# Two layers twice on one core: two tiles of the first layer norm transposed by DMA, halved weight loads, and a newly searched order

## The chip, the core and the metric

The kernel runs on one core of one Trainium2 chip. A core has a matrix engine (TensorE, PE in the profile), a vector engine (VectorE, DVE), a scalar engine (ScalarE, ACT), GpSimd (POOL) and SyncE (SP), which here issues every DMA. The engines run side by side, each through its own list of instructions in order, and wait for each other by semaphores. The metric is the device time of one execution in microseconds (us). Three runs of the kernel before gave 267.95, 268.95 and 270.68 us, a median of 268.95.

## The reference

`x` is 2048 rows of 512 bf16 values. The same two residual layers run twice over:

```python
x = x + _A_ref(_layernorm(x), A_wqkv, A_wo)   # linear attention, 32 heads of 16
x = x + _B_ref(_layernorm(x), B_w1, B_w2)     # relu(x @ w1) @ w2, inner size 1376
x = x + _A_ref(_layernorm(x), A_wqkv, A_wo)
x = x + _B_ref(_layernorm(x), B_w1, B_w2)
```

In `_A_ref`, q, k and v come from one product with `wqkv`. With `phi(t) = where(t > 0, t + 1, exp(t)) + 1e-6`, each head forms `kv = phi(k)^T v` and the sum `z` of `phi(k)` over all rows; the output is `phi(q) kv / (phi(q) z)`, times `wo`. As `kv` and `z` sum over all rows, the second half of a layer A can begin only when the first half has seen every row.

## The kernel before, in words

The 2048 rows are 16 tiles of 128 rows, four tiles to a chunk (`t` = 0 to 3). Layers are numbered 0 to 3 (A, B, A, B), and each layer is a list of steps by chunk; steps of the next layer are woven in when the rows that they need are there. Activations stay in SBUF from the first load to the last store, and so do all weights.

Before a projection a tile is normalised into `xn` (row by row) and then transposed into `Tb`, which has the 512 values of a row along the partitions, in four blocks `c` of 128. There are two ways to transpose. `transpose_pe` has PE multiply four 128x128 blocks by the identity into PSUM (line 600 in the profile), and ACT (line 606) or DVE (line 607) copies the result to `Tb`. `transpose_half` issues one DMA transpose for a pair of tiles on SP's queue (line 586). In layer 0, tiles 0 to 7 go the first way and tiles 8 to 15 the second; in all other layers all tiles go by DMA. In layer B the last 96 columns of the inner activations, `hr`, are also turned by a DMA transpose (`trh`, line 826).

At the start of layer 0, `ln_stats_first` forms mean and variance of a tile on DVE (`bn_stats`, line 534, and `bn_aggr`, line 535); `ln_part_first` makes 1/sqrt(variance), on ACT (lines 540 and 542, Ln and Exp) for tiles 0 to 3 and for the groups of four tiles, on DVE and POOL (lines 545 and 547) for tiles 4 to 7; `ln_norm` writes `xn` on DVE (line 572). `ones_col` then sets the last column of `xn` to 1 on POOL (line 665), since products with `xn` also yield the sums over rows. `warm` issues eight matmuls on zeros before any data is there (line 503), and `warm_fill` four small ones behind the PE transposes of tiles 0 and 1 (line 529). All products of real data stand under line 635, where one helper issues matmul groups.

`a_k(i)` is the K projection of tile i: four matmuls of 512 columns, one for each block `c` of the contraction. `a_q` projects a chunk for q; for chunk 0 `a_q_half` does this in two halves of two tiles each, in 256 columns. `phi` of a projection takes two passes of ACT over PSUM (line 618 linear, line 620 exponential) and two of DVE (lines 622 and 628). `g_r` and `g_a` are products of `phi(k)` with `xn`. `wv_less_last` takes the last row of wv from the rest (DVE, line 661).

Loads are issued by SP in the order of its list: x tiles 0, 1, 2 to 3, then wk (the columns of `wqkv` for k, 512 KB), x 4 to 7, wq, x 12 to 15, x 8 to 11, wv and its last row `wvl`, `wo`, `w1`, and after the first two DMA transposes `w2`. One semaphore belongs to each DMA, so that a user of wk waits for the whole of it.

The order of every engine's list is made by a planner when the kernel is built. `_list_schedule` walks through time with a fixed duration for each operation and picks, within a window of each engine's list, the operation that can start first; ties go by `prio`, the place in the program plus an entry of the table `HINTS`. An entry whose key ends in `!` fixes the engine of an operation that could run on several (`add_flex`). For a DMA the planner takes an issue time on SP's queue (`C_SP_ISSUE`, `C_LOAD_ISSUE`, 1350 ns for `transpose_half`), then 1400 ns, a transfer on one shared channel, 600 ns and an extra `late`. The planner's times decide the order alone; on the chip each instruction waits for its semaphores.

Of the kernel before, what the change touches and what calls it, by code (L numbers as in the profile page):

```python
# [16 lines left out]
C_MM512 = 216.0  # L17
# [26 lines left out]
C_SP_ISSUE = 60.0  # L44
# [10 lines left out]
HINTS = {"0.bnag8": 129, "0.bnst11": -246, "0.bnst12": 104, "0.bnst13": 129, "0.bnst14": 143, "0.bnst15": 144, "0.bnst6": -4,  # L55
# [56 lines left out]

# [1273 lines left out]
```

## Time and profile before

| what | value |
|---|---|
| median of three runs | 268.95 us |
| profiled execution | 268.93 us |
| its span, first to last instruction | 267.2 us |
| around the span | 1.73 us |
| granted TensorE clock | 1.00 |
| PE busy | 262.0 us (98%) |
| DVE busy | 226.2 us (85%) |
| ACT busy | 187.0 us (70%) |
| POOL busy | 58.5 us (22%) |
| first matmul on data (a transpose), first projection | 4.96 us, 6.73 us |
| last matmul starts, last instruction | 263.90 us, 267.2 us |

Busy is the time in which an engine has at least one instruction running. The profile models the end of a matmul, so two matmuls in a row overlap in it; the distance from start to start is what a matmul costs. In a row of a timeline stand the start, the time that the group covers, the engine, the line of the kernel, the operation, the tile written and the tiles read, and how many instructions the row joins; in brackets comes idle time before it and what ended it. In rows of line 635 the first of the tiles read is the one streamed through the array: `ps<-wqkv,Tb` with 512 columns is a K projection, `ps<-Tb,wqkv` a q projection, `ps<-big,xn` belongs to the g products, `ps<-Tb,w` and `ps<-w,Tb` are the first products of layer B. SPq is SP's queue, where a DMA's row is the time that it takes to issue, not to land.

### The profile page before, as it was taken

What the parts mean: (1) busy time and instruction counts of PE and PEld (TensorE: products, weight loads), DVE (VectorE), ACT (ScalarE), POOL (GpSimd) and SP (SyncE); (2) the same over time, 40 slices, a digit from 0 to 9 for tenths busy, and PEclk for the clock granted to TensorE, in tenths of its full rate; (3) what the DMA queues carried; (4) which work ended last, traced back from release to release, by engine and by line L of the source; (5) the groups of instructions that cost most, each with busy time, mean ns of one, the idle gap of its engine ahead of it and who ended that gap; (6) DMA issues with size and microseconds to landing.
All of it is one profiled execution on the core that took longest, in us unless ns stands there. A gap on an engine that the chain in (4) does not pass through costs nothing.

```text
span 267.2 us, 5481 instructions
## 1 busy us (share of the span) xinstructions
PE 262.0 (98%) x2020; PEld 183.1 (69%) x2020; DVE 226.2 (85%) x636; ACT 187.0 (70%) x408; POOL 58.5 (22%) x146
## 2 busy tenths in 40 slices
PE   7999999999989999999999999999999999999995
PEld 3664547644745798857768755674488789888884
DVE  5799974789888999997998675459999999899994
ACT  4998896766975237999667797787899936057400
POOL 3210000026682001403103430000744434000000
PEclk9999999999999999999999999999999999999999
DMA  7986620763765000400400421054373223402003
GB/s 205 368 285 137 197 42 3 157 146 65 86 120 98 2 20 2 89 11 2 79 2 0 79 54 28 2 129 108 62 153 68 39 39 101 81 0 72 28 34 126
DMA packets 44890, 22.18 MB, mean 83 GB/s; under 512 B 34784, under 2 KB 43328, under 8 KB 44864
## 3 DMA queue, kind: packets, MB, share of 16 engines
q1 hardware_dynamic: 44864, 21.83, 34.3%
q8 instruction: 16, 0.26, 0.4%
q14 instruction: 10, 0.08, 0.1%
HBM read 7.14 MB, written 2.10 MB: 35 GB/s over the span
## 4 chain that ended last, share of the span: by engine, by line
PE 92%; ACT 3%; DMA 3%; DVE 1%; SPq 0%; issue 0%; DVEq 0%
PE ps L635 91%; ACT sqscr L650 2%; DMA Tb<-xn 2%; DMA xin<-in_A_x_dram 1%; PE ps L600 1%; ACT xn L581 1%; DVE xres L642 0%; DVE bst L534 0%; PE ps L529 0%; DVE rdc L1064 0%; SPq L471 0%; DVEq L1324 0%; DVE xn L572 0%; ACT big L946 0%
## 5 line engine op out<-in xcount | busy, mean ns | idle before, releaser
L618 ACT ACTIVATE big<-ps 128x512 bf16<-128x512 f32 x64 | 40.7, 644 | 9.5 <-PE ps L635 9.4
L650 ACT ACTIVATE sqscr<-xres 128x512 bf16<-128x512 f32 x48 | 30.0, 625 | 9.1 <-DVE xres L642 5.1
L635 PE MATMUL ps<-Tb,w 128*128 128x256 f16 (+1 forms) x216 | 35.3, 304 | 0.0
L635 PE MATMUL ps<-w,big 128*128 128x256 bf16 (+1 forms) x256 | 32.4, 272 | 0.0
L635 PE MATMUL ps<-wqkv,Tb 128*128 128x512 bf16 x128 | 31.2, 379 | 0.0
L635 PE MATMUL ps<-big,xn 128*128 128x256 bf16 (+1 forms) x224 | 31.1, 288 | 0.0
L635 PE MATMUL ps<-Tb,wqkv 128*128 128x512 f16 (+1 forms) x144 | 30.8, 355 | 0.0
L620 ACT ACTIVATE escr<-ps 128x512 bf16<-128x512 f32 x48 | 29.6, 634 | 1.1 <-PE ps L635 1.1
L635 PE MATMUL ps<-Mf,big 128*128 128x512 bf16 x128 | 29.6, 379 | 0.0
L635 PEld LDWEIGHTS ps<-w,big 128*128 128x128 bf16 (+1 forms) x256 | 24.9, 98 | 3.6 <-ACT big L946 0.3
L635 PEld LDWEIGHTS ps<-big,xn 128*128 128x128 f16 x224 | 21.3, 98 | 8.5 <-issue 0.8
L635 PEld LDWEIGHTS ps<-Tb,w 128*128 128x128 bf16 x216 | 20.6, 98 | 8.8 <-DMA Tb<-xn 0.4
L908 ACT ACTIVATE escr<-ps 128x512 f32<-128x512 f32 (+1 forms) x40 | 20.3, 544 | 8.1 <-PE ps L635 7.4
L895 DVE TENSOR_TENSOR big<-ps,escr 128x512 bf16<-128x512 f32 (+1 forms) x40 | 23.6, 603 | 1.7 <-ACT escr L908 1.1
L564 POOL TENSOR_TENSOR rstd<-veps,nhalf 128x2 f32<-128x2 f32 x24 | 20.4, 853 | 7.9 <-DVE veps L562 6.8
L635 PEld LDWEIGHTS ps<-Tb,wqkv 128*128 128x128 bf16 x144 | 13.7, 98 | 11.7 <-ACT escr L620 0.3
L635 PEld LDWEIGHTS ps<-Mf,big 128*128 128x128 bf16 x128 | 12.3, 98 | 13.8 <-ACT Mf L717 0.2
L622 DVE TENSOR_SCALAR escr<-escr 128x512 bf16<-128x512 bf16 x48 | 13.7, 289 | 8.6 <-ACT escr L620 8.4
L635 PEld LDWEIGHTS ps<-wqkv,Tb 128*128 128x128 f16 x128 | 12.2, 98 | 12.4 <-ACT Tb L606 0.4
L628 DVE TENSOR_TENSOR big<-big,escr 128x512 bf16<-128x512 bf16 x48 | 19.8, 419 | 0.8 <-ACT big L618 0.2
L581 ACT ACTIVATE xn<-xres,nbias,rstd 128x512 f16<-128x512 f32 x21 | 16.8, 815 | 5.1 <-DVE nbias L566 3.9
L898 ACT ACTIVATE big<-big 128x512 bf16<-128x512 bf16 (+1 forms) x31 | 16.2, 542 | 4.8 <-DVE big L895 4.7
(116 smaller groups left out, 515.9 us busy)
## 6 DMA issues: line engine op xcount, KB each, us to landing
big<-rdc SPq DMA_DIRECT2D x32, 128.0 KB, 2.7
wqkv<-in_A_wqkv_dram SPq DMA_DIRECT2D x3, 512.0 KB, 7.0
xin<-in_A_x_dram SPq DMA_DIRECT2D x3, 512.0 KB, 7.8
w<-in_B_w_dram SPq DMA_DIRECT2D x1, 1376.0 KB, 14.5
w<-in_B_w_dram SPq DMA_DIRECT2D x1, 1280.0 KB, 7.0
wo<-in_A_wo_dram SPq DMA_DIRECT2D x1, 512.0 KB, 10.3
out_dram<-GT SPq DMA_DIRECT2D x1, 512.0 KB, 4.1
out_dram<-Mf SPq DMA_DIRECT2D x1, 512.0 KB, 2.6
```

Of the source, the lines that this page charges most:

```text
L564: g.add(POOL, lambda e: e.tensor_tensor(rstd[:, sl], veps[:, sl], nhalf[:, 0:n], ALU.pow), [("veps", lo), ("nhalf",)], [("rstd", i) for i ...
L581: (ACT, lambda e: e.activation(xn[:, i, :], src, ACTF.Identity, scale=rstd[:, i:i + 1], bias=nbias[:, i:i + 1]), C_ACT_SB_AP)],
L600: last = e.transpose(psb()[:, 128 * c:128 * c + 128], xn[:, i, 128 * c:128 * c + 128], ident[:])
L618: g.add(ACT, lambda e: e.activation(dst_ap, psv[:, b, :], ACTF.Identity, bias=1.0 + 1e-6, scale=1.0), [("ps", b)], [dst_key], C_ACT_PSUM, ...
L620: g.add(ACT, lambda e: e.activation(sap, psv[:, b, :], ACTF.Exp), [("ps", b)], skeys, C_ACT_EXP, name=name + "_exp")
L622: g.add(DVE, lambda e: e.tensor_scalar(sap, sap, 1.0, 1e-6, ALU.min, ALU.add), skeys, skeys, C_DVE_BF4X, name=name + "_em")
L628: g.add(DVE, lambda e: e.tensor_tensor(dst_ap, dst_ap, sap, ALU.max), [dst_key] + skeys, [dst_key], 340.0, name=name + "_phi")
L635: last = e.matmul(o, l, r, start=st, stop=sp, skip_group_check=skip)
L650: g.add(ACT, lambda e: e.activation(sqscr[:, q, :], xres[:, i, :], ACTF.Square, scale=math.sqrt(INV_D), accum_out=s2[:, i:i + 1]), xr(i), ...
L895: g.add(DVE, lambda e: e.tensor_tensor(ap, sh(psv[:, bank, 0:w]), sh(other()), ALU.add), [("ps", bank)] + okeys + ([] if first else bk), q ...
L898: g.add_flex([(ACT, lambda e: e.activation(ap, ap, ACTF.Relu), C_ACT_PSUM if len(cs) == 2 else 270.0), (DVE, lambda e: e.tensor_scalar(ap, ...
L908: g.add(ACT, lambda e, w=w: e.activation(q[:, 0:w], psv[:, bank, 0:w], ACTF.Identity), [("ps", bank)], key, C_ACT_PSUM if len(cs) == 2 els ...
```

## The change

- In layer 0, tiles 6 and 7 are no longer transposed by PE. They are normalised as a pair, 1/sqrt(variance) by Ln and Exp on ACT, and one DMA transpose turns both. It is the first transpose and so the one that waits for the loads in `ALL_LOADS` too.
- The second `warm_fill` is left out.
- wk and wq are loaded in two halves of the contraction each (blocks 0 and 1, blocks 2 and 3). The K projections of tiles 0 and 1 and all parts of `a_q_half` become two matmul groups, each waiting for its own half.
- The loads of wv and `wvl` wait for `xn` of tiles 6 and 7, and those of `wo`, `w1` and `w2` for `xn` of tiles 12 to 15.
- The first normalisation of tiles 1 to 7 may be planned on POOL.
- In the planner, the default issue time on SP's queue is 450 ns instead of 60, and that of the transposes of `hr` is 1250 ns; two `late` values differ, and the load times of the halves are half of the whole.
- `HINTS` is another table (474 entries instead of 368), so that the lists of all engines in all four layers are in a new order.

```diff
-C_SP_ISSUE = 60.0
+C_SP_ISSUE = 450.0
+C_TR_ISSUE = 1250.0
...
-         "0.den1": 279, "0.fin12_0": -290, "0.fin13_0": -222, "0.fin6_0": -340, "0.g0_0_3": 73, "0.g0_2_3": 126, "0.g0_3_3":
+         "0.k6_em": -3, "0.k8_phi": -93, "0.k9_phi": 209, "0.kproj9": -485, "0.ld_wka": -100, "0.ld_wkb": -100, "0.ld_wqa":
+         -100, "0.ld_wqb": -99, "0.ld_wvl": 86, "0.ld_x0": -100, "0.ld_x1": -100, "0.ld_x12": -101, "0.ld_x2": -100, "0.ld_x4":
...
-        def ld_w(sl, key):
+        def ld_w(sl, key, cs=slice(0, 4)):
+            dma(lambda e: e.dma_start(wqkv[:, cs, sl], wq_v[:, cs, sl]), [], [(key,)], 370.0 * (cs.stop - cs.start), "ld_" + key,
+                issue=C_LOAD_ISSUE, late=700.0 if key[:2] == "wk" else C_LATE)
...
-        ld_w(slice(D, 2 * D), "wk")
+        ld_w(slice(D, 2 * D), "wka", slice(0, 2))
         ld_x(2, 4)
-        ld_w(slice(0, D), "wq")
+        ld_w(slice(D, 2 * D), "wkb", slice(2, 4))
+        ld_w(slice(0, D), "wqa", slice(0, 2))
+        ld_w(slice(0, D), "wqb", slice(2, 4))
...
+        def tied(load, names):
+            n = len(g.ops)
+            load()
+            for o in g.ops[n:]:
+                o.sdeps += [p for p in g.ops[:n] if p.name in names and p not in o.sdeps]
+
+        def loads_a():
...
+        def loads_b():
...
-            if hi <= FIRST_ACT_TILES or hi - lo == 4:
+            if hi <= FIRST_ACT_TILES or hi - lo >= 2:
...
-                g.add(DVE, lambda e: e.tensor_scalar(xn[:, i, :], xin[:, i, :], mv[:, i, 0:1], rstd[:, i:i + 1], ALU.subtract, ALU.mult),
-                      [("xin", i), ("mean", i), ("rstd", i)], [("xn", i)], C_DVE_NORM_BF, name="norm%d" % i)
+                f = (lambda e: e.tensor_scalar(xn[:, i, :], xin[:, i, :], mv[:, i, 0:1], rstd[:, i:i + 1], ALU.subtract, ALU.mult))
+                g.add_flex([(DVE, f, C_DVE_NORM_BF)] + ([(POOL, f, C_POOL_NORM)] if 0 < i < 8 else []),
+                           [("xin", i), ("mean", i), ("rstd", i)], [("xn", i)], name="fnorm%d" % i)
...
-            if i < 2:
+            if i < 1:
                 warm_fill(i)
...
+            parts = ((0, 1, "wka"), (2, 3, "wkb")) if first_k and i < 2 else ((0, 1, 2, 3, "wka", "wkb"),)
...
+                for k, key in enumerate(("wqa", "wqb")):
...
-                [("hr", s)], [("big", u)], 450.0, "trh%d" % t)
+                [("hr", s)], [("big", u)], 450.0, "trh%d" % t, issue=C_TR_ISSUE)
...
-                if t < FIRST_PE_CHUNKS:
+                if t < FIRST_PE_CHUNKS and i < 6:
...
+            if t == 1:
+                ln_part_first(6, 8)
+                ln_norm(6, True)
+                ln_norm(7, True)
+                tr_dma(1, 1)
...
+            if t == 1:
+                tied(loads_a, ["fnorm6", "fnorm7"])
...
+                        if t + 3 == NCH - 1:
+                            tied(loads_b, ["fnorm%d" % i for i in range(NT - 4, NT)])
```

More of the change, by code (lines that the diff above doesn't have):

```diff
@@ L52 @@
 WINDOW = {PE: 64, ACT: 80, DVE: 80, POOL: 12, SP: 6}
-HINTS = {"0.bnag8": 129, "0.bnst11": -246, "0.bnst12": 104, "0.bnst13": 129, "0.bnst14": 143, "0.bnst15": 144, "0.bnst6": -4,
[56 rows of a table removed]
+HINTS = {"0.bnag15": 26, "0.bnag3": 137, "0.bnag9": 130, "0.bnst12": 51, "0.bnst13": 223, "0.bnst15": 189, "0.bnst3": -18,
[80 rows of a table added]
 class _Op:
@@ L465, in ld_x @@
             dma(lambda e: e.dma_start(xin[:, lo:hi, :], x_v[:, lo - 1:hi - 1, :]), [], [("xin", i) for i in range(lo, hi)],
-                350.0 * (hi - lo), "ld_x%d" % lo, issue=C_LOAD_ISSUE, late={1: 100.0, 2: 200.0}.get(lo, C_LATE))
+                350.0 * (hi - lo), "ld_x%d" % lo, issue=C_LOAD_ISSUE, late={1: 100.0, 2: 650.0}.get(lo, C_LATE))
         wq_v = A_wqkv.rearrange("(c p) n -> p c n", p=128)
-        def ld_w(sl, key):
-            dma(lambda e: e.dma_start(wqkv[:, :, sl], wq_v[:, :, sl]), [], [(key,)], 1480.0, "ld_" + key, issue=C_LOAD_ISSUE, late=500.0 if key == "wk" else C_LATE)
+        def ld_w(sl, key, cs=slice(0, 4)):
+            dma(lambda e: e.dma_start(wqkv[:, cs, sl], wq_v[:, cs, sl]), [], [(key,)], 370.0 * (cs.stop - cs.start), "ld_" + key,
+                issue=C_LOAD_ISSUE, late=700.0 if key[:2] == "wk" else C_LATE)
@@ L471, in build_kernel @@
         dma(lambda e: e.dma_start(xin[:, 0, :], x_h), [], [("xin", 0)], 370.0, "ld_x0", issue=C_LOAD_ISSUE, late=-350.0)
         ld_x(1, 2)
-        ld_w(slice(D, 2 * D), "wk")
+        ld_w(slice(D, 2 * D), "wka", slice(0, 2))
         ld_x(2, 4)
-        ld_w(slice(0, D), "wq")
+        ld_w(slice(D, 2 * D), "wkb", slice(2, 4))
+        ld_w(slice(0, D), "wqa", slice(0, 2))
+        ld_w(slice(0, D), "wqb", slice(2, 4))
         for t in range(1, NCH):
             ld_x(4 * t, 4 * t + 4)
-        ld_w(slice(2 * D, 3 * D), "wv0")
@@ L479, in build_kernel @@
-        dma(lambda e: e.dma_start(wvl[:], A_wqkv[D - 1:D, 2 * D:3 * D].broadcast_to([128, D])), [], [("wvl",)], 2000.0, "ld_wvl",
-            issue=C_LOAD_ISSUE)
-        dma(lambda e: e.dma_start(wo[:], A_wo.rearrange("(c p) n -> p c n", p=128)), [], [("wo",)], 1500.0, "ld_wo", issue=C_LOAD_ISSUE)
         nfull = NFC - 1 if FLAST < 128 else NFC
-        dma(lambda e: e.dma_start(w1[:], B_w1.rearrange("(c p) n -> p c n", p=128)), [], [("w1",)], 4500.0, "ld_w1", issue=C_LOAD_ISSUE)
-        dma(lambda e: e.dma_start(w2[:, 0:nfull, :], B_w2[0:nfull * 128, :].rearrange("(c p) n -> p c n", p=128)),
-            [], [("w2a",)], 5500.0, "ld_w2a", issue=C_LOAD_ISSUE)
@@ L487, in build_kernel @@
-        if FLAST < 128:
-            dma(lambda e: e.dma_start(w2[0:FLAST, NFC - 1, :], B_w2[nfull * 128:DFF, :]), [], [("w2b",)], 600.0, "ld_w2b", issue=C_LOAD_ISSUE)
+        def tied(load, names):
[4 more added lines that the diff above has]
+        def loads_a():
+            ld_w(slice(2 * D, 3 * D), "wv0")
+            dma(lambda e: e.dma_start(wvl[:], A_wqkv[D - 1:D, 2 * D:3 * D].broadcast_to([128, D])), [], [("wvl",)], 2000.0, "ld_wvl",
+                issue=C_LOAD_ISSUE)
@@ new lines, in loads_b @@
+        def loads_b():
+            dma(lambda e: e.dma_start(wo[:], A_wo.rearrange("(c p) n -> p c n", p=128)), [], [("wo",)], 1500.0, "ld_wo", issue=C_LOAD_ISSUE)
+            dma(lambda e: e.dma_start(w1[:], B_w1.rearrange("(c p) n -> p c n", p=128)), [], [("w1",)], 4500.0, "ld_w1", issue=C_LOAD_ISSUE)
+            dma(lambda e: e.dma_start(w2[:, 0:nfull, :], B_w2[0:nfull * 128, :].rearrange("(c p) n -> p c n", p=128)),
+                [], [("w2a",)], 5500.0, "ld_w2a", issue=C_LOAD_ISSUE)
+            if FLAST < 128:
+                dma(lambda e: e.dma_start(w2[0:FLAST, NFC - 1, :], B_w2[nfull * 128:DFF, :]), [], [("w2b",)], 600.0, "ld_w2b", issue=C_LOAD_ISSUE)
@@ L489, in build_kernel @@
         W2KEYS = [("w2a",), ("w2b",)] if FLAST < 128 else [("w2a",)]
-        ALL_LOADS = [("wk",), ("wq",)]
+        ALL_LOADS = [("wka",), ("wkb",), ("wqa",), ("wqb",)]
         def _table(e):
@@ L651, in sq, with a_k @@
                   xr(i), [("sqscr", q), ("s2", i)], C_ACT_SQ, name="sq%d" % i)
-        def a_k(i):
+        def a_k(i, first_k=False):
             b = alloc_bank()
-            mm_group(lambda: [(psv[:, b, :], Tb[:, i, c, :], wqkv[:, c, D:2 * D], c == 0, c == 3, False) for c in range(4)],
-                     [("T", i), ("wk",)], [("ps", b)], 4 * C_MM512, "kproj%d" % i)
+            parts = ((0, 1, "wka"), (2, 3, "wkb")) if first_k and i < 2 else ((0, 1, 2, 3, "wka", "wkb"),)
+            for k, p in enumerate(parts):
+                cs = [c for c in p if isinstance(c, int)]
+                mm_group(lambda cs=cs: [(psv[:, b, :], Tb[:, i, c, :], wqkv[:, c, D:2 * D], c == 0, c == 3, False) for c in cs],
+                         [("T", i)] + [(c,) for c in p if not isinstance(c, int)], [("ps", b)], len(cs) * C_MM512,
+                         "kproj%d" % i if len(parts) == 1 else "kproj%d_%d" % (i, k))
             phi_evac(b, pk_tile(i), ("big", pk_unit(i)), "k%d" % i, stt=(i % 4) < K_STT)
@@ L729, in a_q @@
                                             c == 0, c == 3, False) for c in range(4)],
-                         [("T", i) for i in range(4 * t, 4 * t + 4)] + [("wq",)], [("ps", b)], 4 * C_MM512, "qproj%d_%d" % (t, j))
+                         [("T", i) for i in range(4 * t, 4 * t + 4)] + [("wqa",), ("wqb",)], [("ps", b)], 4 * C_MM512, "qproj%d_%d" % (t, j))
                 q_evac(t, j, b, first)
@@ L740, in a_q_half @@
                 i0 = 4 * t + 2 * h
-                mm_group(lambda b=b, j=j: [(psv[:, b, 256 * h:256 * h + 256], wqkv[:, c, 128 * j:128 * j + 128], Tb[:, i0:i0 + 2, c, :],
-                                            h == 0 and c == 0, c == 3, True) for c in range(4)],
-                         [("T", i0), ("T", i0 + 1), ("wq",)], [("ps", b)], 4 * C_MM256, "qh%d_%d_%d" % (t, h, j))
+                for k, key in enumerate(("wqa", "wqb")):
+                    mm_group(lambda b=b, j=j, k=k: [(psv[:, b, 256 * h:256 * h + 256], wqkv[:, c, 128 * j:128 * j + 128], Tb[:, i0:i0 + 2, c, :],
+                                                     h == 0 and c == 0, c == 3, True) for c in (2 * k, 2 * k + 1)],
+                             [("T", i0), ("T", i0 + 1), (key,)], [("ps", b)], 2 * C_MM256, "qh%d_%d_%d_%d" % (t, h, j, k))
                 if h == 1:
@@ L1165, in p1 @@
                     for i in range(4 * t, 4 * t + 4):
-                        a_k(i)
+                        a_k(i, first_layer)
                         if first_layer and t == 0 and i % 2 == 1:
```

133 rows, old and new, of the table HINTS are left out of this document.

## The prediction

> **What bounds the kernel now.** I read the page's totals and slices first, then the chain of waits, then the timeline of PE around each place where the chain leaves PE.
>
> ```profile
> PE 262.0 (98%) x2020; PEld 183.1 (69%) x2020; DVE 226.2 (85%) x636; ACT 187.0 (70%) x408; POOL 58.5 (22%) x146
> PE   7999999999989999999999999999999999999995
> PEclk9999999999999999999999999999999999999999
> ```
>
> PE has 5.2 us without work in 267.2, at full granted clock. Start-to-start inside the stream is 0.216 us for a 512-column matmul and 0.109 for 256, so a busy PE here is a PE at its rate. The change can win only what it takes off PE's list, an earlier start, or a hole. The chain of waits shows the holes (start, us, what):
>
> ```profile
> 6.79 0.98 PE ps L635 x4
> 7.77 0.22 PE ps L600 x4
> ...
> 71.67 0.18 ACT big L946
> 71.85 4.67 DMA Tb<-xn
> 76.51 0.05 issue
> 76.56 187.63 PE ps L635 x1544
> 264.19 0.02 issue
> ```
>
> Line 635 is every projection and product, line 600 the PE transposes. From 76.56 to the end PE is never short of work. In the part cut out, the chain runs through PE from 4.96 to 62.94 and then over ACT and DVE, while PE itself goes on with other products. So there are two places: the start, and 71.85 to 76.51. First the start, by the timeline (start, us, what) and by the rows of tile wqkv:
>
> ```profile
> 2.18 0.43 SPq L470 DMA_DIRECT2D wqkv<-in_A_wqkv_dram  x1
> 5.61 0.60 ACT L606 ACTIVATE Tb<-ps 128x512 f16<-128x512 f16 x1
> 6.40 0.39 PE L529 MATMUL ps<-wrm 128*128 128x128 bf16 x4
> 6.73 1.04 PE L635 MATMUL ps<-wqkv,Tb 128*128 128x512 bf16 x4
> ...
> DMA to landing us min/median/max: 4.5/7.0/9.1
> ```
>
> wk is issued at 2.18 and lands 4.5 us later, at 6.69; the first K projection starts at 6.73, although its Tb tile was out of PSUM at 6.21. So wk, not the transpose, sets the start of the dense stream. Now the hole, by PE's timeline and by the DMA view of 71 to 75 us (slices of 0.1 us):
>
> ```profile
> 69.51 6.23 PE L635 MATMUL ps<-Tb,w 128*128 128x512 f16 x36
> 76.56 0.85 PE L635 MATMUL ps<-w,Tb 128*128 128x96 bf16 x16 [0.83 <-DMA Tb<-xn]
> ```
> ```profile
> GB/s 205 202 212 202 205 136 64 241 156 200 202 215 169 138 60 20 8 0 0 0 0 0 3 8 8 10 10 10 8 10 10 11 0 28 161 192 218 205 207 210
> q8 instruction: 1, 0.02, 2.4%
> ```
>
> Between 72.4 and 74.3 the transposes move next to nothing. A 16 KB instruction packet starts at 71.75 and takes 1.54 us, just before. The transpose issued at 69.15 lands after 5.12 us, the one at 71.85 after 4.66; undisturbed ones take 3.04 to 3.40. PE's matmul before the hole is followed 1.205 us later by the next, 0.99 over its rate. That is the only hole over 0.15 us after 6.73.
>
> **The change, part by part**, against the profiled execution's own 268.93 us (span 267.2 and 1.73 around it; the median of the runs is 268.95, so both count the same).
>
> *wk and wq in halves.* By the hints the loads go x0, x1, wka, x2, wkb, wqa, x4, wqb, x12, x8. x2 (256 KB, third in the queue) landed at 4.81, so wka, of the same size in its place, lands there too, and T0 (6.21) releases the first two matmuls. They can start when trp1's four end, about 6.40, and run to 6.83. The bytes up to wkb equal those up to wk before, so wkb lands at 6.69 and the second pair ends at 7.27 instead of 7.60: **-0.33**. Bounds: -0.43 (no wait at all), and +0.13 if one more issue (0.46) delays wkb by its whole length. x2 lands 0.93 later (two back-to-back 256 KB loads), so xn2 comes at about 7.9 instead of 6.99; trp2 stands behind kproj1, until 8.14. T3 slips to about 9.5, and PE would miss 0.5 us, but the wqa halves of q (0.87 us, landed near 7.5 where wq came at 10.15) are there to fill it. If the order puts them elsewhere, 0.5 is lost.
>
> *Fill 1 and the PE transposes of 6 and 7 go.* The fill ran in the shadow of wk: nothing. Eight transposes at 0.056 us, with PE full before and behind them (0.22 us a tile in the chain): **-0.44**. DVE loses two copies (0.41 and 0.42).
>
> *Tiles 6 and 7 by DMA.* PE reached kproj6 at 19.7; now it will at 18.9. One transpose of a pair takes 1.34 us of SP's queue and 3.04 to 3.40 to land, so xn6 and xn7 must be there by about 15.6. Before, they were written at
>
> ```profile
> 17.74 0.40 DVE L572 TENSOR_SCALAR xn<-xin,mv,rstd 128x512 f16<-128x512 bf16 x1
> 18.54 0.38 DVE L572 TENSOR_SCALAR xn<-xin,mv,rstd 128x512 f16<-128x512 bf16 x1
> ```
>
> DVE is 96 to 100% busy from 10 to 20, but 2.56 us of that are four bn_stats from 14.87 on, ahead of these norms and wanted by later tiles; POOL, nearly idle, may take norms (0.77 us for its f32 form at line 576). Moving them is enough: 0 for this part, bounds 0 and +3.3 (below). The pair's Ln and Exp cost ACT 0.40 to 0.92, hidden by ACT's own waits for PE at 20.59 and 30.53 (0.75, 0.90); without these they would delay PE by as much. SP's wait for xn6/7 holds the tied wv and wvl behind it: issued near 17, back-to-back transfers 1.3 and 1.2, landed by about 21, used by DVE at 23.98. wo to w2 wait for xn15 (31.5): SP is through with them near 38, the bytes near 44; first users 48.28 (wo), 63.72 (w1), 74.06 (w2); the spreads come at 45.29. Cover everywhere, 1 us at the spreads.
>
> *The order.* The new constants only steer the planner. It had 60 ns for issuing a transpose of h; the trace has 1.19 to 1.28. The instruction packets number 16 for PE's 2020 matmuls and 2020 weight loads, one in about 252. PE's list is 24 instructions shorter (16 of the transposes, 8 of the fill), so the packet of 71.75 comes 12 pairs, 2.6 us, later in the work. In the old order that lies between two transposes. I take the hole as gone: **-0.99**, bounds 0 and -0.99. The Trainium skill ("Runtime: NRT & Kernel Launch", Instruction fetch mechanics) says code is refilled in blocks of 256 instructions and that crossing one is mostly hidden. For PE the trace agrees; for the transposes it does not, and by the rule the hole would have another cause and stay, 268.7.
>
> A new order also brings misses of its own. Six PE waits on transposes besides the hole end within 0.1 us of the landing; such landings spread by 0.36 us. From none to 6 x 0.36 = 2.2; the old order, without the hole, left about 0.3 (0.11 at 9.60, 0.13 at 113.8, less elsewhere). Nearest to that row: **+0.5**.
>
> Sum: 268.93 - 0.33 - 0.44 - 0.99 + 0.5 = **267.7**, that is 0.5% less. One per cent, 2.7 us, is about what a measurement of this kernel can tell from no change.
>
> **Rivals.**
>
> *A. The hole stays*, since a code packet meets another pair that PE waits for. For it: sixteen packets and 36 transposes; against it: one of the sixteen cost PE a hole. 268.93 - 0.77 + 0.5 = 268.7.
>
> *B. Many small misses.* The whole list was searched anew, against planned durations; against it, the old order's six tight waits lost 0.3 between them. With 2.2: 268.93 - 0.77 - 0.99 + 2.2 = 269.4, more if a bank or ACT is late behind each.
>
> *C. T6 and T7 come late; slower.* If xn6/7 stay behind the four bn_stats, at 18.92, the pair lands at 18.95 + 3.3 = 22.25, and PE, whose other work is used up (the g products of chunk 0, 2.17 us, are spent by then), stands from 18.9: 3.3 us. 268.93 - 0.77 + 3.3 = 271.5, or 270.5 with the hole gone; I take 271. It decides from an issue at 16.4 on (loss over 0.77), with the hole gone from 17.4.
>
> *D. The clock.* Matmuls run at half rate (0.427 for 512 columns) until 6.40, at full rate after, in spite of 0.33 us idle before 4.96. If the missing fill kept the clock low over two K projections, 8 x 0.21 = 1.7: 269.4. Against it: PE will now go from trp1 straight into kproj0, and the 0.83 us hole at 76 changed no rate. The Trainium skill ("TensorE: Matmul & The Clock Gate", What's actually happening) has the clock rise after some 3.4 us of sustained work; here it took 5.2, so a fill can matter.
>
> *E. The halves bring nothing* (wkb 0.4 late): 268.0, within the forecast's own range.
>
> **How the numbers follow.** Forecast with E 0.45 (own range 266.6 to 268.4), A 0.22, B 0.16, C 0.13, D 0.04. Faster by over 1% (under 266.2) needs every gain, no miss and a shorter tail: 0.06, out of the forecast. Slower by over 1% (over 271.6): half of C, a third of B: 0.12. Within: 0.82. The range runs from 266.6 (all bounds at their best give 268.93 - 0.43 - 0.44 - 1.2 = 266.9, and the runs scatter) to 270.7, which leaves out most of C.
>
> **What would show it.** First K projection at about 6.4 in two pairs, the second done by 7.3. No line 600 work after tile 5; one transpose on SP's queue issued before 16, landed by 19, and no PE wait on Tb near 19. PE's waits on Tb between 70 and 80 gone. From the last hole to the end PE without waits, and the last matmul near 262.5. It is wrong if PE waits over 1 us in a place where it did not before: look at kproj6, and at the first products after each change of layer.

## The result, and the profile after

The changed kernel takes 280.96 us, the median of six runs (280.81 to 281.19), against 268.38 us for the kernel before, measured beside it: a ratio of 1.0454, with a 95% interval of 1.0418 to 1.0490. The forecast was 267.7 us with a range up to 270.7. The kernel became 4.5% slower, and none of the rivals had named the cause.

The totals and slices of the page after, to be held against those of before:

```profile
PE 264.2 (95%) x1991; PEld 183.4 (66%) x2008; DVE 226.8 (81%) x628; ACT 199.3 (71%) x418; POOL 58.9 (21%) x152
PE   5659799999999999999999999999999999999995
DVE  3257689658999899989978977518999999988994
ACT  6899999887589333689993489677799857438300
PEclk9579999999999999999999999999999999999999
```

After the sixth slice, which ends at 42 us, the profile has a single wait of PE, of 0.16 us; all is lost ahead of that. There ACT is full, PE is empty for up to half of a slice and DVE for more, and PE's clock was granted at half from 7.4 to 14.3 and from 17.7 to 21.1 us. ACT is busy for 12.3 us more than before, with 10 instructions more (199.3 us and 418 against 187.0 and 408). The groups of ACT's instructions tell which (line, engine, operation, count, busy us and mean ns, idle before):

```profile
L577 ACT ACT_TABLE_LOAD x6 | 7.7, 1283 | 0.9 <-PEq L1423 0.8
L579 ACT ACT_TABLE_LOAD x4 | 5.1, 1283 | 0.1
L658 ACT ACT_TABLE_LOAD x2 | 2.6, 1283 | 0.0
L530 ACT ACT_TABLE_LOAD x1 | 1.3, 1283 | 0.0
```

The kernel before has one such row, of one load:

```profile
L493 ACT ACT_TABLE_LOAD x1 | 1.3, 1283 | 1.0 <-POOL nhalf L507 1.0
```

Thirteen table loads stand where there was one. Line 577 is Ln, line 579 Exp, line 658 the exponential of `phi`. The kernel's own load (line 493 before, 530 after) brings in a set that holds both functions. Before, it is the first thing that ACT does. After, it comes at 38.72 us, and ahead of it the compiler put a load of its own wherever ACT goes from Ln to Exp or back. The chain of waits of the kernel after, from 0 to 40 us (start, us, what), shows that these loads are the path:

```profile
...
3.72 0.19 DVE mv L572
3.94 0.20 ACT veps L577
4.16 1.28 ACT L579
5.45 0.20 ACT rstd L579
5.67 1.28 ACT L577
6.96 0.20 ACT veps L577
7.18 1.28 ACT L579
8.48 0.21 ACT rstd L579
8.72 0.42 DVE xn L609
9.19 0.62 PE ps L638 x4
9.83 0.60 ACT Tb L644
10.45 1.28 ACT L577
11.74 0.20 ACT veps L577
11.96 1.28 ACT L658
...
```

The third tile is not yet normalised at 14 us; before, the fourth was at 8.0. Why the load was late stands in the diff, in the table of hints, which has 528 entries after the change (not 474, as the list of changes has it) and carries this one for the load (the kernel before has none):

```diff
+         "0.spread3_3": -129, "0.sq1": 314, "0.sq2": 261, "0.sq9": 279, "0.table": 432, "0.tr3_1": -33, "0.trev4!": 0,
```

It moves the operation `table` 432 places down in priority. For the planner this is harmless: an activation has a fixed duration there, whatever set is loaded.

### The profile page after: what moved, and what is told of

It is laid out like the page before. It is cut to its first block, busy times and chain, and to the rows that moved or that the text cites. A ratio compares the mean times of both kernels' runs of the same rounds, so it can differ in the third digit from the quotient of the medians.

```text
span 279.2 us, 5455 instructions
## 1 busy us (share of the span) xinstructions
PE 264.2 (95%) x1991; PEld 183.4 (66%) x2008; DVE 226.8 (81%) x628; ACT 199.3 (71%) x418; POOL 58.9 (21%) x152
## 3 DMA queue, kind: packets, MB, share of 16 engines
HBM read 7.14 MB, written 2.10 MB: 33 GB/s over the span
## 4 chain that ended last, share of the span: by engine, by line
PE 82%; ACT 11%; DVE 4%; issue 1%; DMA 1%; DVEq 0%
PE ps L673 82%; ACT L577 2%; ACT big L656 2%; ACT L579 2%; ACT escr L658 1%; ACT Tb L644 1%; ACT xres L658 1%; ACT L658 1%; DMA xin<-in_A_x_dram 1%; DVE xn L1008 1%; DVE big L666 1%; DVE big L938 0%; ACT veps L577 0%; DVE Tb L1008 0%; DVE escr L660 0%
## 5 line engine op out<-in xcount | busy, mean ns | idle before, releaser
L656 ACT ACTIVATE big<-ps 128x512 bf16<-128x512 f32 x64 | 39.2, 638 | 4.6 <-PE ps L673 4.5
L673 PE MATMUL ps<-Tb,wqkv 128*128 128x512 f16 (+1 forms) x144 | 33.0, 367 | 0.0
L673 PEld LDWEIGHTS ps<-big,xn 128*128 128x128 f16 x224 | 21.1, 98 | 11.8 <-ACT escr L658 2.5
L673 PE MATMUL ps<-Mf,big 128*128 128x512 bf16 x123 | 28.5, 379 | 0.3
L951 ACT ACTIVATE escr<-ps 128x512 f32<-128x512 f32 (+1 forms) x40 | 21.4, 562 | 8.5 <-PE ps L673 8.3
L660 DVE TENSOR_SCALAR escr<-escr 128x512 bf16<-128x512 bf16 x48 | 13.9, 296 | 12.9 <-ACT escr L658 12.8
L673 PEld LDWEIGHTS ps<-Tb,wqkv 128*128 128x128 bf16 x144 | 14.5, 103 | 12.9 <-issue 1.1
L673 PEld LDWEIGHTS ps<-wqkv,Tb 128*128 128x128 f16 x128 | 12.8, 103 | 14.2 <-issue 2.2
L941 ACT ACTIVATE big<-big 128x512 bf16<-128x512 bf16 (+1 forms) x31 | 17.9, 598 | 5.4 <-DVE big L938 5.4
L601 POOL TENSOR_TENSOR rstd<-veps,nhalf 128x2 f32<-128x2 f32 x24 | 18.5, 772 | 14.9 <-DVE veps L599 14.2
L673 PEld LDWEIGHTS ps<-Mf,big 128*128 128x128 bf16 x128 | 12.3, 98 | 14.0 <-ACT Mf L759 0.4
L593 POOL TENSOR_SCALAR mean<-s 128x2 f32<-128x2 f32 x24 | 7.5, 312 | 57.0 <-DVE xres L680 55.0
```

The lines of the kernel that those rows point to most:

```text
L593: g.add(POOL, lambda e: e.tensor_scalar(mean[:, sl], s1[:, sl], -INV_D, None, ALU.mult), [("s1", i) for i in tl], [("mean", i) for i in tl ...
L601: g.add(POOL, lambda e: e.tensor_tensor(rstd[:, sl], veps[:, sl], nhalf[:, 0:n], ALU.pow), [("veps", lo), ("nhalf",)], [("rstd", i) for i ...
L656: g.add(ACT, lambda e: e.activation(dst_ap, psv[:, b, :], ACTF.Identity, bias=1.0 + 1e-6, scale=1.0), [("ps", b)], [dst_key], C_ACT_PSUM, ...
L660: g.add(DVE, lambda e: e.tensor_scalar(sap, sap, 1.0, 1e-6, ALU.min, ALU.add), skeys, skeys, C_DVE_BF4X, name=name + "_em")
L673: last = e.matmul(o, l, r, start=st, stop=sp, skip_group_check=skip)
L941: g.add_flex([(ACT, lambda e: e.activation(ap, ap, ACTF.Relu), C_ACT_PSUM if len(cs) == 2 else 270.0), (DVE, lambda e: e.tensor_scalar(ap, ...
```

## The experiments

**The table load moved back to the head.** The theory: the late load is the whole loss. The rivals: the new order or the DMA changes lose the time, or the half clock does. The changed kernel with only that operation moved in ACT's list, after planning, so that nothing else changes its place:

```diff
         order, total = _list_schedule(g.ops, g.tile_ops, vbank)
+        tb_op = [o for o in order[ACT] if o.name == "table"][0]
+        order[ACT].remove(tb_op)
+        order[ACT].insert(0, tb_op)
...
```

> The changed kernel with one operation moved: the op `table` (load of the table set that holds both Ln and Exp) stands first in ACT's list as before the change; the order of everything else, all four layers, is that of the changed kernel, which runs 13 table loads on ACT (12 of them ahead of the Ln, Exp and phi of layer 0) where the kernel before runs one. Theory T, the late table load is the whole loss: the 12 loads go, PE starts the first K projection near 6.4 us and is back at full clock by then, and the time is that of the forecast without this, 267.7 us (266.6 to 268.6), a ratio of 0.993 to 1.001 to the kernel before. Rival R, the new order or the DMA changes lose the time and the table loads lie beside it: 275 us or more. Rival C, the half clock near 9 to 21 us is a cause of its own (left-out fill): first projections still at 0.427 us each, 270 to 272.

Measured: 268.57 us (268.05 to 269.24, 12 runs), a ratio to the kernel before of 0.9992 (0.9974 to 1.0009). All 12.4 us are back with one operation. ACT has one load again:

```profile
L530 ACT ACT_TABLE_LOAD x1 | 1.3, 1283 | 1.1 <-POOL nhalf L544 1.1
```

The clock is at full from 6.35 us on, so the half clock came with the late load and not with the left-out fill. What is left is no gain either: the forecast had put this kernel 0.9 us lower. Where that went is read from its trace, below.

**The late load in the kernel before.** The same fault without any other part of the change: `table` is moved behind the 1/sqrt of tiles 8 to 11.

```diff
         order, total = _list_schedule(g.ops, g.tile_ops, vbank)
+        tb_op = [o for o in order[ACT] if o.name == "table"][0]
+        order[ACT].remove(tb_op)
+        k8 = [k for k, o in enumerate(order[ACT]) if o.name == "rstd8"][0]
...
+        order[ACT].insert(k8 + 1, tb_op)
```

> The kernel before, with the op `table` moved behind the 1/sqrt of tiles 8 to 11 in ACT's list, and nothing else. The compiler then puts in ten table loads of 1.28 us ahead of the Ln and Exp of tiles 0 to 3 and 8 to 11 and the phi between. Theory T: the loss of the changed kernel comes without any of its other parts; the first of the loads is hidden behind the wait for x0, six lie in the chain of tiles 1 to 3, the rest before the phi: +8 to +12 us, 276 to 280. Rival R (loads hidden beside PE, which is the bound): within 2 us of the kernel before.

Measured: 281.15 us (280.61 to 282.13), a ratio of 1.0461 (1.0431 to 1.0491), a little over the top of what was expected. The groups of ACT in this kernel:

```profile
L540 ACT ACT_TABLE_LOAD x5 | 6.4, 1283 | 0.9 <-PEq L1376 0.8
L542 ACT ACT_TABLE_LOAD x4 | 5.1, 1283 | 0.1
L620 ACT ACT_TABLE_LOAD x1 | 1.3, 1283 | 0.0
L493 ACT ACT_TABLE_LOAD x1 | 1.3, 1283 | 0.0
```

Ten loads more than before are 12.8 us on ACT, and 12.3 us are lost. With the run above this settles the loss: the late load alone makes it, on either kernel, and moving it to the head removes it.

**The entry left out, planned anew.** The same change without `"0.table": 432`, so that the planner makes new lists.

> The changed kernel without the one entry of the table of hints that puts `table` late (432 places), planned anew: SP's order stays, some 400 rows of DVE's and 260 of PE's list stand elsewhere. Theory T: as the kernel with the op moved by hand, 266.6 to 269; any difference between the two is what a replanned order with hints made for another plan costs, up to 1.5 us. Rival R: 275 or more.

Measured: 269.73 us (268.95 to 271.04, 12 runs), a ratio of 1.0027 (1.0004 to 1.0049). The loss is gone here too, but this order is 1.2 us slower than the one with the operation moved by hand, and just measurably slower than the kernel before. The hints were made for a plan with the entry in it; without it some lists come out otherwise, and the list of PE's waits has three more on DVE, of 0.2 to 0.4 us. Where all of the 1.2 us goes was not followed.

**What an early table load costs.** `table` stands third, behind Ln and Exp of tile 0:

```diff
+        k0 = [k for k, o in enumerate(order[ACT]) if o.name == "rstd0"][0]
...
+        order[ACT].insert(k0 + 1, tb_op)
```

> The changed kernel with the op `table` behind the Ln and Exp of tile 0 in ACT's list: three table loads in all, the first hidden as in the changed kernel, the second between Ln and Exp of tile 0, the third behind it. It prices an early load. Theory T (a load in the chain of the first tiles moves the whole stream by its length): 1.3 us for the second, 0 to 1.5 for the third, so 1.3 to 2.8 over the kernel with the op moved to the head, 269 to 270.5. Rival (loads cost time only when ACT's total becomes the bound): no more than 0.5 over it.

Measured: 271.66 us (270.93 to 271.86), 3.1 over the kernel with the load first, more than two loads (2.57). PE's timeline of this kernel shows the rest:

```profile
6.09 0.61 PE L638 MATMUL ps<-ident,xn 128*128 128x128 f16 x4 [1.26 <-DVE xn L609]
...
8.34 3.62 PE L673 MATMUL ps<-wqkv,Tb 128*128 128x512 bf16 x8
11.75 1.71 PE L673 MATMUL ps<-Tb,wqkv 128*128 128x256 f16 x8
```

The first K projection starts at 8.34 instead of 6.21. After the waits ahead of it PE is at half rate until 13.12: the eight matmuls take 0.427 us each instead of 0.216, 1.7 more, and six or so of the next eight 0.1 more each. Against this the waits for wq, 1.6 us in the kernel with the load first, are covered. 2.1 + 1.7 + 0.7 - 1.6 is 2.9, and the span is 2.8 longer. So a hole of PE ahead of the dense stream costs again in clock, which the forecast had as a rival for another reason (the fill left out; that cost nothing).

**Where the rest of the forecast went.** PE's waits and the start of its timeline in the kernel with the table first:

```profile
PE ps L673 <- DMA wqkv<-in_A_wqkv_dram: 1.3, 2, 0.7
```
```profile
6.21 2.09 PE L673 MATMUL ps<-wqkv,Tb 128*128 128x512 bf16 x8
8.97 1.05 PE L673 MATMUL ps<-Tb,wqkv 128*128 128x256 f16 x8 [0.67 <-DMA wqkv<-in_A_wqkv_dram]
9.85 0.61 PE L638 MATMUL ps<-ident,xn 128*128 128x128 f16 x8
11.09 0.61 PE L673 MATMUL ps<-Tb,wqkv 128*128 128x256 f16 x4 [0.63 <-DMA wqkv<-in_A_wqkv_dram]
```

The halves of wq land at 8.92 and 11.05 and PE stands for both; start to start the two holes lose 0.83 and 0.80 over PE's rate. In this execution nearly all of the expected gain is given back here. To see whether x 4 to 7, issued between the two halves, takes their bandwidth, its load is put behind them:

```diff
+        names = [o.name for o in order[SP]]
+        x4 = order[SP].pop(names.index("ld_x4"))
+        order[SP].insert([o.name for o in order[SP]].index("ld_wqb") + 1, x4)
...
```

> The changed kernel with `table` at the head of ACT's list, and SP's load of x tiles 4 to 7 moved behind the second half of wq; nothing else. In the kernel with the table first, PE stood 0.67 us for the first half of wq (landed 8.92) and 0.63 for the second (11.05), although 256 KB back to back had been put at some 0.8 us, 7.5 and 10.15. Theory: x4 (512 KB), issued between them, shares the queue with the first half. Then wqa lands near 7.9 and wqb near 9, both waits of PE go, x4 lands 0.7 later (11.0 for 10.35), and of the 1.6 us lost there 0.5 to 1.3 come back: 267.3 to 268.1, a ratio of 0.994 to 0.998 to the kernel before. Rival: the early halves are late by themselves (small descriptors), wqa still lands after 8.5, and the time is the same as with the table first, or longer since x4 is later.

Measured: 268.80 us (268.33 to 269.37, 12 runs), a ratio of 1.0003 (0.9979 to 1.0026): neither what the theory expected nor longer. The theory of the landings is borne out in part: wqb lands at 9.31, 1.7 earlier, wqa at 8.52, 0.4 earlier. But the wait has only moved:

```profile
7.27 1.47 PE L673 MATMUL ps<-wqkv,Tb 128*128 128x512 bf16 x6 [0.34 <-DMA wqkv<-in_A_wqkv_dram]
...
14.67 0.40 PE L638 MATMUL ps<-ident,xn 128*128 128x128 f16 x4 [0.93 <-DVE xn L609]
```

Now tile 4 is late. In these two orders the first 14 us hang on the loads whichever comes first. The landings also differ between executions: wqa landed at 7.53 to 8.92 in six profiles with the same loads in the same order, and the 8.92 is that of the kernel with the table first. How much of the last tenths is due to this stays open.

**The hole at 75 us.** The forecast laid it to an instruction packet that met the transposes. Here the kernel before gets more instructions in PE's list (68 by its trace, 73 by the expectation), waits that have long been met, so that the packet comes earlier; the compiler gives one instruction for two such waits:

```diff
+        PAD = {"qproj3_"} | {"fin%d_" % i for i in range(13)}
...
                 for (o, l, r, st, sp, skip) in mk():
+                    if pad:
+                        e.wait_ge(sem_eng[DVE], 1)
+                        e.wait_ge(sem_eng[POOL], 1)
                     last = e.matmul(o, l, r, start=st, stop=sp, skip_group_check=skip)
```

> The kernel before, with 73 waits more in PE's list, all on counts long reached, spread over q projections of chunk 3 and final products of layer 0 (two waits on a matmul of 512 columns give one instruction of 51 ns beside 216 ns of matmul). No order, no data and no transfer changes. Theory F (an instruction packet of PE blocks the DMA transposes that run beside it): the packet of 71.75 us starts near 67.5, between two transposes; the transposes issued at 69.15 and 71.85 land after 3.0 to 3.4 us (5.12 and 4.66 before), PE's wait on Tb at 75.7 is gone and the time is 0.7 to 1.0 us less, a ratio of 0.996 to 0.9975. Rival (the slow transposes come from the transpose of h between them): both still take over 4.5 us and the wait stays; time the same or up to 0.5 longer for the waits.

Measured: 267.83 us (267.58 to 268.06, 12 runs), a ratio of 0.9974 (0.9956 to 0.9992). The packet starts at 68.74 and is over before the transpose issued at 69.22 moves its first byte. The rows of tile Tb from 60 to 80 us, first of the kernel before, then of this one:

```profile
DMA to landing us min/median/max: 3.0/3.2/5.1
```
```profile
DMA to landing us min/median/max: 3.0/3.0/3.2
```

PE's wait on Tb is gone from its list of waits, and the span is 1.0 us shorter. Of all kernels tried this is the fastest, by the addition of instructions that do nothing.

The other direction, on the kernel with the table first: 88 and then 60 such instructions by the traces (94 and 65 by the expectations), to bring its packet of 77.66 us onto the transpose issued near 70. The edit is the same, with K projections 14 and 15, two of the g products and the final products 0 to 13 for the first, and the q projections of chunk 3 with final products 0 to 10 for the second.

> The kernel with the table first, with 94 such waits more in PE's list. No order and no data changes. Theory F: the instruction packet of 77.67 us starts near 70.5, on the transpose issued at 70.31 that PE takes up within 0.05 us of its landing at 73.34; it lands 1 to 2 us later and PE stands for 0.7 to 2 us, 269.3 to 270.6. Rival: landing and time as in the kernel with the table first, within 0.4 us.

Measured: 268.55 us (267.94 to 269.09), a ratio of 0.9996 (0.9971 to 1.0020). The packet started at 69.83 and took 0.95 us; the transpose, issued at 69.78, moved its bytes after that and landed in 3.10. The packet missed, so this tells nothing between the theories.

> The kernel with the table first, with 65 waits more in PE's list, since with 94 the instruction packet (69.83 us) was over before the transpose issued at 69.78 moved its first bytes. No order and no data changes. Now the packet should start 1.2 to 1.8 us after the issue of that transpose, with its bytes (they run from 1.2 to 2.7 us after the issue). Theory F: the packet takes 1.4 us or more instead of 0.95, the transpose lands 4 us or more after its issue instead of 3.0 to 3.1, and PE, whose wait ended 0.03 us after the landing, stands for 0.3 to 1.5 us: a span of 267.2 to 268.8 (266.8 to 267.4 with the packet elsewhere). Rival (a packet alone does not block a transpose; before the change it met two transposes and one of h back to back): it lands within 3.4 us and no wait of PE appears between 70 and 78.

Measured: 270.85 us (270.60 to 271.21), a ratio of 1.0075 (1.0056 to 1.0094). At the place aimed at the packet (70.78, 0.95 us long) was early again; the transpose issued at 70.09 landed after 3.57, and PE had no hole. But the added instructions shift all later packets too, and two of those met transposes that PE was waiting for, at 152.69 and 191.96. PE's waits, its timeline at the first of the two, and the DMA view of 150 to 156 us (slices of 0.15 us):

```profile
PE ps L680 <- DMA Tb<-xn: 2.4, 2, 1.3
```
```profile
152.84 0.60 PE L680 MATMUL ps<-big,xn 128*128 128x256 bf16 x4
154.78 1.90 PE L680 MATMUL ps<-wqkv,Tb 128*128 128x512 bf16 x8 [1.35 <-DMA Tb<-xn]
```
```profile
GB/s 0 0 0 0 0 0 135 225 218 210 208 213 195 186 118 116 217 292 237 84 61 0 0 0 7 10 9 10 9 130 295 285 136 0 0 0 0 0 0 48
...
q8 instruction: 1, 0.02, 1.0%
```

From 153.15 to 154.35 the view has 10 GB/s or less, much like the 11 or less of 72.6 to 74.3 before the change. The transpose issued at 149.73 lands after 5.01 us, that of 190.67 after 4.66; in the kernel of the test before, which has the same order, they took 3.19 and 3.05. The two holes are 2.4 us and the time is 2.3 us over that kernel's. No order and no data differ between these two kernels, only the number of waits that were long met, and with it the place of the packets. So that a packet can stall transposes is shown, at places other than the one aimed at.

All ten traces together say more about when. They hold 367 transposes. 294 landed without a packet beside them, and none of these took over 3.92 us; all 21 that took 4 us or more had one. Where the packet started 1.1 to 2.0 us after the transpose was issued, all ten landed late, after 3.97 to 4.66 us. From 2.2 to 3.1 us after the issue it was 10 of 31, and what decides there is open. Where it started earlier, only two of 32 took 4 us or more, and both had been issued right behind transposes that were held up. The packet aimed at the transpose of 70.09 started 0.69 after it.

## Why the prediction was wrong, step by step

*The step that failed* is the order: "The new constants only steer the planner", with "from none to 6 x 0.36 = 2.2" as bounds of what a new order can cost, and the loads' order read from the hints. The hints that were read for the loads also hold the entry that moves `table`. Its operation has a price in the trace of before, the one ACT_TABLE_LOAD of 1.28 us that is hidden behind the wait for x0. The prediction priced a new order as if it could only make waits longer. An order can also change which instructions there are: with the load of the common set late, the compiler added twelve, 15.4 us of ACT, all but the first of them on the chain that feeds PE, and 12.4 us were lost where the bound was 2.2. ACT's spare time at 20.59 and 30.53, named as cover for the pair's Ln and Exp, was gone: from 10 to 30 us ACT was busy for 19.8 of 20. The Trainium skill ("ScalarE: Activation LUTs", Table sets: the hidden batching unit) has one set with both exp and ln, one load for both; the trace of the kernel with the table first, which has a single load, agrees. The Trainium skill ("ScalarE: Activation LUTs", What ACT_TABLE_LOAD costs) puts a switch of sets at a load of about 1.28 us and a drain of about 1.38. Here the load took 1.28, began 0.02 behind the activation ahead of it, and the next activation began 0.01 after it, so no drain was paid.

The other steps are read on the kernel with the table first, 268.57 us.

- *wk in halves, -0.33*: right here. The first projection starts at 6.21 (6.40 forecast), its second pair waits for wkb (landed at 6.79), and the second projection is done near 8.14, as worked out. In the two kernels with added waits on top wkb came at 7.14 and 7.29, which took 0.3 and 0.4 of it.
- *The wqa halves as cover*: mis-sized. They were put at "near 7.5"; here they landed at 8.92, and wqb at 11.05 instead of 10.15. The price of that cover gone was put at 0.5; in this execution, 0.4 us over the kernel's median, it is 1.6. In the three profiles of the kernel planned anew and of those with added waits wqa came at 7.82 to 8.38 and wqb at 10.44 to 10.70, and the two cost 0.8 to 1.2. So this term alone takes back from half to nearly all of the gain.
- *Eight PE transposes less, -0.44, and the fill*: they are gone from PE's list, and the fill's place costs nothing (full clock from 6.35 us on).
- *Tiles 6 and 7*: right. The transpose is issued at 14.16 (before 16 was asked), lands at 17.37, and PE has no wait there. Rival C did not occur; wv, wo and w1 were never waited for.
- *The hole at 75 gone, -0.99*: right in the result, PE has no wait on Tb. The cause, a packet of instructions, was argued; the kernels with added waits bear it out. Where the packet would go was wrong: it starts at 77.66, 5.9 us later than before and not 2.6. At 71.75 + 2.6 it would have started 1.6 us after the transpose issued at 72.76 in the new order, in the stretch where all ten landed late. So that it missed is luck in part. The Trainium skill ("Runtime: NRT & Kernel Launch", Instruction fetch mechanics) calls the crossing of a block mostly hidden. For PE's own list the traces agree; for the transposes they do not: one packet cost PE 0.99 us before the change, two cost 2.4 in the last kernel above.
- *Misses of the new order, +0.5*: about right. Behind 14.8 us the small gaps between matmuls sum to 2.7 us in the two profiles of this order with the table at the head that kept all matmul records and met no stalled transpose, against 2.3 before the change without its hole. The one wait of 0.2 on DVE in the list of the kernel with the table first is in the main a matmul that its trace lacks.
- *The range*: its best case, 266.9, takes off 1.2 for the hole, which is the whole distance between the two matmuls; the hole's own bound of 0.99 gives 267.1. Nothing hangs on it.

-0.33 - 0.44 - 0.99 + 1.63 + 0.4 is 0.3 us slower; the profiled executions differ by 0.1 the same way (269.0 and 268.93). Without the late load the change is worth nothing that can be measured.

## What to carry to other kernels

Where a planner orders activations, the load of the table set is part of the order. It should stand fixed ahead of the first activation and out of the search's reach, and the number of ACT_TABLE_LOAD rows is the first thing to compare between two orders. When a diff replaces a table of hints, look for every entry that is new and touches an operation with a side effect on others, before weighing the rest. And a load split to come earlier must be placed in the whole queue: with 512 KB issued between the halves of wq the second landed 2.1 to 2.9 us after the first, and 0.8 after it without.

## What the runs showed that was not expected

An instruction packet of PE, 16 KB, one for about 252 of its instructions, can hold up the DMA transposes by up to 2 us: their rate falls from over 200 GB/s to about 10, and one that starts 1.1 to 2.0 us after the issue of a transpose did so in all ten cases. Adding 68 waits that wait for nothing made a kernel 0.26% faster (0.08 to 0.44), and 60 left another 0.75% slower than the kernel before (0.56 to 0.94), where 88 had left it at the same time; what differs is where these packets fall. A difference of some tenths of a per cent between two orders can therefore come from where the packets fall. The half clock also came back by itself: PE stood for 1.3 and 0.8 us in the first 8 us, and its next eight matmuls of 512 columns ran at half rate, 0.427 us instead of 0.216.
